# A fused attention and gated-MLP block on one core: V and the output projection in 64x128 tiles, weights loaded into both partition halves, new instruction lists

## The chip, the core and the metric

The kernel runs on one core of a Trainium2 chip. A core has TensorE (matmuls and transposes; PE in the profile, its weight loads PEld), VectorE (DVE), ScalarE (ACT) and GpSimd (POOL), and SyncE (SP), which here only issues DMAs. Each takes its instructions in the order of its own list and waits on semaphores for the others. Matmul operands lie in SBUF on 128 partitions; results go to PSUM, which has eight banks of 2 KB per partition. The metric is device time in microseconds (us) of one execution, lower is better.

## What is computed

2048 tokens x of width 448 in bf16; a dilated local attention, then a gated MLP that mixes over tokens:

```python
# attention: 16 heads of 28, window W = 8, dilation 2
q, k, v = layernorm(x) @ wqkv
idx = s - 2 * arange(8)                      # masked where negative
h = x + (softmax(q . k[idx] * 28**-0.5) @ v[idx]) @ wo
# gMLP: F = 1792, Fh = 896
z = gelu(layernorm(h) @ w_in)
z1, z2 = z[..., :Fh], layernorm(z[..., Fh:])
g = w_sp @ z2 + b_sp[:, None]                # over the tokens, 2048 x 2048
out = h + (z1 * g) @ w_out
```

## The kernel before

The tokens are split into two halves s of 1024. A unit u (0 to 7) is the blocks u and u + 8 of 128 tokens, one of each half. LayerNorm 1 of a unit takes, per block, a bn_stats (L818) and a bn_aggr (L819) on VectorE, a reciprocal root on POOL (L808, L809) or ScalarE (L830, L831), and a normalising tensor_scalar (L838). The unit is then transposed into xh: on TensorE with a copy out of PSUM (L854; units 0 to 2), or by a transposing DMA of SP (L845; units 3 to 7, and all units of LayerNorm 2). In xh, partition 64*s + f holds feature f of a 64-feature chunk c (seven chunks) of half s. So a matmul with 64 rows works on one half, and two such matmuls, one per half, run beside each other in the array. Each needs its weights on the same 64 partitions, so every weight is wanted in both partition halves. Before, each of wq, wk, wv and w_in is loaded into partitions 0 to 63 and copied into the others by VectorE or ScalarE (L803, L805; "cp" and "cpw" tasks). wq and wk come to a staging area in z2p and are spread from 28 to 32 columns per head on the way.

q and k are made in pieces of tokens per half: 0 to 128, 128 to 256, 256 to 512, 512 to 1024 (k runs 14 further back for the halo, from a separately normalised xhalo). The matmuls are 64x128 (L965), two groups of 128 columns to a task in the narrow pieces.

Attention goes in nine tiles of 114 queries per half. As the dilation is 2, even and odd tokens do not meet; each tile is handled by parity w, 64 keys and 58 query columns each. V of a tile (L1005) is made in four 64x64 tiles, half s by parity w, with every second token of xh as the stationary operand. Then come logits (L1040, 32x64 tiles), exp (L1053), a mask (L1060), row sums (L1069) and the product with V (L1089, both 64x32 tiles), ln and exp(-ln) of the sums (L1077, L1099), and the scaling "ot" (L1107), which writes over qT. There four heads lie on 128 partitions, so the output projection "y" (L1143) takes for each block four full 128x128 matmuls of 448 columns. "h" (L1151) adds x.

LayerNorm 2 follows per unit, then z2 (L1163, 64x128 tiles), gelu (L1173), LayerNorm 3 (L1179 to L1193); z1 (L1207) and its gelu (L1217); then g (L1244), bias and gate (L1254, L1262) and the output (L1273, L1281, L1285). The last stage is a dense run of 448 full matmuls for g and 112 for the output.

What order all this runs in is written out: `SEQ` holds five lists of task numbers, for SP, POOL, VectorE, ScalarE and TensorE. `replay` walks them with assumed durations only to choose PSUM banks and buffers, and semaphores are made from reads and writes. PSUM is taken in four pairs of banks by q, k, V, logits, sums, products, y, z2 and z1. The lists of before put the weight loads on ScalarE's queue (k, then q, and V later) and hold back all x blocks of units 2 to 7 until block 8 has landed. On TensorE they run unit 0 and 1 transposes, the eight narrow q and k tasks, the unit 2 transpose, then V and logits of tiles 0 and 1, the 256-wide pieces, and so on; the last q and k piece starts after tile 2's logits.

Of the kernel before, what the change touches and what calls it, by code (L numbers as in the profile page):

```python
# [24 lines left out]
QW = ST + 4  # L25

BF16 = mybir.dt.bfloat16
F32 = mybir.dt.float32
I32 = mybir.dt.int32
# [5 lines left out]
WPEN = 200  # L35
MPEN = 10.704
OFF = {"q": -124.25, "v": 1265.42, "evv": 569.01, "l": -1263.94, "exp": -259.78, "mask": -1085.83, "r": -1027.56, "o":
       -1264.27, "ln": 1046.18, "ot": 511.44, "y": -65.14, "h": 108.86, "ln2": -195.97, "z2": -1857.43, "ge": 2334.62,
       "n3": 1020.58, "x0": -60.60, "xd": 242.96, "evq": 1087.78, "cp": 975.37, "td": 561.22, "cw": -627.08}
ADJ = ()  # L40
SEQ = (
# [30 lines left out]
)  # L72
O_AFTER_LN = True
NBANKS = 8
TU = 26.48
NE = 2
NL = 2
NV = 3
SET_E = "natural_log_exp_and_others"
SET_G = "gelu_apprx_tanh_and_others"  # L80

# [122 lines left out]
class Task:  # L204
    __slots__ = ("name", "eng", "dur", "emit", "deps", "prio", "acq", "rel", "mode", "epoch",
                 "gate", "nbytes", "start", "end", "succ", "ndep", "rt", "nmm", "alts", "bw", "setup", "waits", "mark")

    def __init__(self, name, eng, dur, emit, deps=(), prio=0.0, acq=(), rel=(), mode=None,
                 epoch=None, gate=None, nbytes=0, nmm=0, alts=None):
        self.name = name  # L210
        self.eng = eng
        self.dur = dur
        self.emit = emit
        self.deps = [d for d in deps if d is not None]
        self.prio = prio
        self.acq = list(acq)
        self.rel = list(rel)
        self.mode = mode
        self.epoch = epoch
        self.gate = gate  # L220
        self.nbytes = nbytes
        self.nmm = nmm
        self.bw = 215.0
        self.setup = 2.0
        self.waits = []
        self.mark = None
        self.alts = alts
        self.start = self.end = None
        self.succ = []
        self.ndep = 0  # L230
        self.rt = 0.0


class Planner:


    ENGS = ("sp", "pool", "dve", "act", "pe")

    def __init__(self, pools, epochs, table_task, marker):
        self.tasks = []  # L240
        self.named = {}
        self.filler = None
        self.marker = marker
        self.pools = {k: [(0.0, s) for s in v] for k, v in pools.items()}
        self.epochs = epochs
        self.table_task = table_task
# [7 lines left out]
    def pick(self, p, n):  # L254

        free = {s: f for f, s in self.pools[p]}
        if p != "ps":
            return sorted(sorted(free, key=lambda s: (free[s], s))[:n]) if len(free) >= n else None
        whole = sorted((b for b in range(0, 32, 2) if b in free and b + 1 in free), key=lambda b: max(free[b], free[b + 1]))
        if n == 1:  # L260
            single = sorted((s for s in free if s ^ 1 not in free), key=lambda s: free[s])
            if single:
                return [single[0]]
# [1079 lines left out]
```

## Time and profile before

| | us |
|---|---|
| median of 3 runs | 246.23 (245.85 to 247.01) |
| profiled execution, first to last instruction | 247.4 |
| profiled execution's own time around that span | not recorded |
| TensorE busy | 232.1 (94%) |
| VectorE, ScalarE, POOL busy | 143.3, 91.4, 28.8 |
| first q matmul starts | 12.38 |
| last q and k piece starts | 40.17 |
| z1 starts | 93.26 |
| g starts | 126.5 |

In the profile a row is a line of the kernel, the engine and the operation, with what it writes and reads, its shape, and how often it occurs; then its busy time and the mean time of one. Engines overlap, so busy times do not add up to the span. The chain that ended last is followed back from the last instruction, at each step to what it waited for. A row of a stretch gives its length, then busy time and number of instructions for PE, PEld, DVE, ACT and POOL, then the granted TensorE clock (1.00 is full), the DMA engines' mean share and GB/s. Matmuls overlap in the array: one of 448 columns takes 349 ns from start to end while the next starts 94 to 190 ns after it, so work is counted from start to next start.

### The profile page before, as it was taken

How to read it: one execution, taken by the hardware profiler on the slowest of the kernel's cores; microseconds unless marked ns; L12 is line 12 of the kernel's file. 1: busy time of each engine (PE TensorE's matmuls, PEld its weight loads, DVE VectorE, ACT ScalarE, POOL GpSimd, SP SyncE). 2: the span in 40 equal slices, each digit the busy share in tenths (PEclk: the TensorE clock that was granted, in tenths of full speed). 3: DMA queues.
4: the chain of work that ended last, by engine and by line, in shares of the span. 5: the costliest groups of instructions: out<-in, count | busy, mean ns of one | idle time of the engine just before them, and what ended most of it. 6: DMA issues, size and time to landing. Idle time of an engine off the chain costs nothing.

```text
span 247.4 us, 6649 instructions
## 1 busy us (share of the span) xinstructions
PE 232.1 (94%) x3004; PEld 123.7 (50%) x3004; DVE 143.3 (58%) x281; ACT 91.4 (37%) x103; POOL 28.8 (12%) x69
## 2 busy tenths in 40 slices
PE   0399799999999999999999999999999999999995
PEld 0297485445556555555544444444444444444442
DVE  6697847779999897798970022335021407541743
ACT  2668784886979965575740000000000000000000
POOL 2843010000021112104530000000000000000000
DMA  6935965893224976886733333100000000010113
GB/s 159 255 80 61 138 91 98 128 154 71 46 40 85 152 197 124 180 147 150 108 85 85 87 85 85 42 3 0 0 0 0 3 0 0 2 46 29 56 57 111
DMA packets 54436, 20.02 MB, mean 81 GB/s; under 512 B 46584, under 2 KB 54280, under 8 KB 54408
## 3 DMA queue, kind: packets, MB, share of 16 engines
q1 hardware_dynamic: 52584, 18.05, 37.4%
q10 hardware_dynamic: 1824, 1.55, 2.8%
q8 instruction: 23, 0.38, 0.7%
q14 instruction: 5, 0.04, 0.1%
HBM read 6.39 MB, written 1.84 MB: 33 GB/s over the span
## 4 chain that ended last, share of the span: by engine, by line
PE 93%; DMA 3%; issue 1%; ACT 1%; ACTq 1%; DVE 0%
PE psum L1244 39%; PE psum L965 11%; PE psum L1163 9%; PE psum L1273 9%; PE psum L1207 9%; PE psum L1005 5%; PE psum L1143 5%; DMA z2p<-in_A_wqkv_dram 3%; PE psum L1040 3%; PE psum L1089 2%; PE psum L1069 1%; ACT reg L803 1%; ACTq L723 1%; ACT xh L803 0%; ACTq L730 0%
## 5 line engine op out<-in xcount | busy, mean ns | idle before, releaser
L1254 DVE TENSOR_TENSOR ub<-psum,reg 128x512 bf16<-128x512 f32 x28 | 18.8, 687 | 64.3 <-PE psum L1244 64.2
L1244 PE MATMUL psum<-reg,z2p 128*128 128x512 bf16 x224 | 50.0, 379 | 0.0
L1244 PE MATMUL psum<-wspT_lo,z2p 128*128 128x512 bf16 x224 | 49.0, 379 | 0.0
L1244 PEld LDWEIGHTS psum<-wspT_lo,z2p 128*128 128x128 bf16 x224 | 21.8, 98 | 26.6 <-issue 0.4
L1244 PEld LDWEIGHTS psum<-reg,z2p 128*128 128x128 bf16 x224 | 21.9, 98 | 26.1
L965 PE MATMUL psum<-xh,reg 64*128 64x128 bf16 (+3 forms) x448 | 28.5, 290 | 2.8 <-issue 2.0
L965 PEld LDWEIGHTS psum<-xh,reg 64*128 64x128 bf16 x448 | 19.4, 105 | 10.5 <-issue 3.4
L1163 PE MATMUL psum<-w_in,xh 64*128 64x448 bf16 x224 | 22.5, 349 | 0.0
L1273 PE MATMUL psum<-reg 128*128 128x448 bf16 x112 | 22.3, 352 | 0.0
L1207 PE MATMUL psum<-xh,w_in 64*128 64x512 bf16 x196 | 22.2, 376 | 0.0
L818 DVE BATCH_NORM_STATS2 st<-x_tm 128x6 f32<-128x448 bf16 x32 | 19.5, 609 | 1.0 <-DMA x_tm<-in_A_x_dram 0.8
L1179 DVE BATCH_NORM_STATS2 st<-z2p 128x6 f32<-128x448 bf16 x32 | 17.7, 612 | 2.6 <-ACT z2p L1173 2.5
L803 ACT ACTIVATE reg<-psum 128x896 bf16<-128x896 f32 (+3 forms) x21 | 16.8, 824 | 5.8 <-PE psum L965 4.2
L1053 ACT ACTIVATE reg<-psum 128x928 bf16<-128x928 f32 x18 | 16.1, 943 | 6.4 <-PE psum L1040 6.4
L1281 DVE TENSOR_TENSOR tring<-psum,x_tm 128x448 bf16<-128x448 f32 x16 | 9.6, 616 | 14.0 <-PE psum L1273 14.0
L808 POOL TENSOR_SCALAR rs<-mv 128x2 f32<-128x2 f32 x21 | 6.3, 300 | 93.7 <-DVE mv L819 78.4
L1173 ACT ACTIVATE z2p<-psum 128x896 bf16<-128x896 f32 x16 | 14.2, 916 | 6.8 <-PE psum L1163 6.8
L1163 PEld LDWEIGHTS psum<-w_in,xh 64*128 64x128 bf16 x224 | 11.9, 94 | 9.5 <-issue 0.9
L1217 ACT ACTIVATE reg<-psum 128x1024 bf16<-128x1024 f32 x14 | 13.7, 1030 | 7.8 <-PE psum L1207 7.8
L1273 PEld LDWEIGHTS psum<-reg 128*128 128x128 bf16 x112 | 11.0, 98 | 10.6
L1207 PEld LDWEIGHTS psum<-xh,w_in 64*128 64x128 bf16 x196 | 11.1, 94 | 9.7
L809 POOL TENSOR_TENSOR rs<-rs,nhalf 128x2 f32<-128x2 f32 x21 | 15.6, 743 | 1.8
(63 smaller groups left out, 201.2 us busy)
## 6 DMA issues: line engine op xcount, KB each, us to landing
out_dram<-tring SPq DMA_DIRECT2D x16, 112.0 KB, 1.7
x_tm<-in_A_x_dram SPq DMA_DIRECT2D x13, 112.0 KB, 5.7
w_in<-in_B_w_in_dram SPq DMA_DIRECT2D x2, 448.0 KB, 5.5
z2p<-in_A_wqkv_dram ACTq DMA_DIRECT2D x2, 392.0 KB, 6.3
reg<-in_B_w_out_dram SPq DMA_DIRECT2D x1, 784.0 KB, 4.8
w_in<-in_B_w_in_dram SPq DMA_DIRECT2D x2, 336.0 KB, 5.1
reg<-in_B_b_sp_dram SPq DMA_DIRECT2D x1, 512.0 KB, 4.2
reg<-in_A_wo_dram SPq DMA_DIRECT2D x4, 98.0 KB
```

Of the source, the lines that this page charges most:

```text
L803: iss("act", lambda e: e.activation(dst, src, AF.Copy), reads=rd, writes=wr)
L809: iss("pool", lambda e: e.tensor_tensor(dst, dst, nh, ALU.pow), reads=rr + [r_nhalf], writes=rr)
L818: iss("dve", lambda e: e.bn_stats(st[:, b, :], x_tm[:, b, :]), reads=[r_x[b]], writes=[rl[b]])
L965: iss("pe", lambda e, c=c, s=s, gi=gi, lhs=lhs: e.matmul(psum[:, bk[s] * 512 + cw * gi:bk[s] * 512 + cw * gi + cw], lhs, xh[64 * s:64 * s ...
L1053: iss("act", lambda e: e.activation(E[:, es[0], 2 * n:2 * n + 2, :], pair_view(lb, 0, 8 * JW), AF.Exp, scale=SCALE), reads=[r_bank[lb[0]], ...
L1163: iss("pe", lambda e, c=c, s=s: e.matmul(psum[:, zb[s] * 512:zb[s] * 512 + D], xh[64 * s:64 * s + 64, c, HX + 128 * u:HX + 128 * u + 128], ...
L1173: iss("act", lambda e: e.activation(z2p[:, u:u + 9:8, D * k:D * k + D], pair_view(zb, 0, D), AF.Gelu_apprx_tanh), reads=[r_bank[zb[0]], r_ ...
L1179: iss("dve", lambda e, b=b: e.bn_stats(st3[:, b, k, :], z2p[:, b, D * k:D * k + D]), reads=[r_z2[b][k]], writes=[r_st3[b][k]])
L1207: iss("pe", lambda e, c=c, s=s: e.matmul(psum[:, bk[s] * 512:bk[s] * 512 + 512], w_in[64 * s:64 * s + 64, c, 128 * f:128 * f + 128], xh[64 ...
L1244: iss("pe", lambda e, b=b: e.matmul(psum[:, gb[0] * 512:gb[0] * 512 + 512], z2p[:, b, 128 * f:128 * f + 128], src[:, b, 512 * (tc % 2):512 ...
L1254: iss("dve", lambda e: e.tensor_tensor(ub[:, us_[0], :], psum[:, gb[0] * 512:gb[0] * 512 + 512], bb[:, 512 * tc:512 * tc + 512], ALU.add), ...
L1273: iss("pe", lambda e, f=f: e.matmul(psum[:, wb[0] * 512:wb[0] * 512 + D], z1p[f][:, 128 * m:128 * m + 128], w_out[:, f, :], start=(f == 0) ...
```

## The change

1. V: VectorE or ScalarE first copies a tile's 128 tokens of xh into a small buffer xv, even tokens first. TensorE then takes 14 matmuls of 64x128 for V instead of 28 of 64x64.
2. Output projection: the two halves of the tokens get their own 64 partitions in oT (two heads each), wo is loaded twice (wo2), and y takes 16 matmuls of 64x128 instead of 8 of 128x128. Row sums and the product with V write to the matching partitions; the row sums of tile 0 take 8 matmuls instead of 16.
3. wq, wk, wv and w_in are loaded by two DMAs each, one per partition half. For wq, wk and wv one comes from SP and one from ScalarE's queue. The copies between halves go; four spreading copies for q and k stay, over 128 partitions.
4. q and k come in three pieces: 0 to 256, 256 to 512, 512 to 1024.
5. The mask is applied per half of the heads (two instructions for one); logits use 28 rows instead of 32; two bn_aggr stand together behind both bn_stats.
6. xhalo and thalo move into the staging area, ub into attention's region, memsets of wo and thalo from VectorE to POOL. The older search code goes.
7. The lists are new. Read by names, SP issues x0, x1, xhalo, x6, wq (half 0), x3, x10, wk (half 0), seven more x blocks, wv (half 0), wo1, x13, then the transposing DMA of unit 3, x4, and those of units 7, 4, 5, 6, then w_in, wo and w_sp loads. ScalarE issues x9, x8 and the other halves of wq, wk and wv, with two reciprocal roots between the last two. VectorE: bn of blocks 0, 9, 1, 8, the halo, normalise, copy of q, halo, xh of unit 0, copy of k, then bn of other units, parity copies of tiles 0, 3 and 2 and the remaining normalises. TensorE: transposes of units 1 and 0, q and k of the first piece, V of tile 0, the unit 2 transpose, logits of tiles 1 and 0, the second piece with V of tiles 1 and 3 in between, row sums and products of tiles 0 and 1, V of tile 2, the last piece. Tiles then run in pairs (2 and 3, 5 and 4, 6, 8, 7) up to z2.

```diff
+CQ = [0, 256, 512, ST]
+CK = [0, 256, 526, ST + HALO]
...
+        def ld_w(p):
             c0 = "qkv".index(p) * D
+            t_w[p] = [dma(eng, "w%s%d" % (p, s), lambda e, s=s: e.dma_start(
+                w_ld[p][64 * s:64 * s + 64], A_wqkv[:, c0:c0 + D].rearrange("(c p) n -> p c n", p=64)),
+                D * D * 2, writes=[r_ld[p][s]], issue=0.65, bw=350.0) for s, eng in ((0, "sp"), (1, "act"))]
...
-                if p == "v":
-                    copy(tk[0].eng, wv[64:128], wv[0:64], [r_st[p]], [r_w[p][1]])
-                else:
-                    copy(tk[0].eng, wpd[p][64 * h:64 * h + 64, :, 256 * j:256 * j + 256].rearrange("p c (h d) -> p c h d", d=32)[:, :, :, 0:DH],
-                         w_st[p][:, :, 224 * j:224 * j + 224].rearrange("p c (h d) -> p c h d", d=DH), [r_st[p]], [r_w[p][h][j]])
+                    copy(tk[0].eng, wpd[p][:, :, 256 * j:256 * j + 256].rearrange("p c (h d) -> p c h d", d=32)[:, :, :, 0:DH],
+                         w_ld[p][:, :, 224 * j:224 * j + 224].rearrange("p c (h d) -> p c h d", d=DH), r_ld[p], [r_w[p][j]])
...
+            def em(a=a, xs=xs, rx=rx, tk=tk):
+                o = HX - HALO + a
+                copy(tk[0].eng, xv[:, xs[0], :, :].rearrange("p c (w j) -> p c w j", w=2),
+                     xh[:, :, o:o + 128].rearrange("p c (j w) -> p c w j", w=2), rx, [r_xv[xs[0]]])
...
                 for c in range(NC7):
-                    for w in range(2):
-                        for s in range(2):
-                            iss("pe", lambda e, c=c, s=s, w=w: e.matmul(
-                                psum[64 * w:64 * w + 64, bk[s] * 512:bk[s] * 512 + D],
-                                xh[64 * s:64 * s + 64, c, HX - HALO + a + w:HX - HALO + a + w + 127:2],
-                                wv[64 * s:64 * s + 64, c, :], start=(c == 0), stop=(c == NC7 - 1),
-                                tile_position=(64 * s, 64 * w)),
...
+                    for s in range(2):
+                        iss("pe", lambda e, c=c, s=s: e.matmul(
+                            psum[:, bk[s] * 512:bk[s] * 512 + D],
+                            xv[64 * s:64 * s + 64, xs[0], c, :],
+                            wv[64 * s:64 * s + 64, c, :], start=(c == 0), stop=(c == NC7 - 1)),
...
-                for s in range(2):
-                    for g in range(4):
-                        iss("pe", lambda e, s=s, g=g: e.matmul(psum[:, bk[s] * 512:bk[s] * 512 + D],
-                                                              qT[:, s, g, 128 * u:128 * u + 128], wo_p[:, g, :],
-                                                              start=(g == 0), stop=(g == 3)),
+                for x in range(8):
+                    for s in range(2):
+                        iss("pe", lambda e, s=s, x=x: e.matmul(psum[:, bk[s] * 512:bk[s] * 512 + D],
+                                                              oT[64 * s:64 * s + 64, x, 128 * u:128 * u + 128],
+                                                              wo2[64 * s:64 * s + 64, x, :],
+                                                              start=(x == 0), stop=(x == 7)),
```

More of the change, by code (lines that the diff above doesn't have):

```diff
@@ L78 @@
 NV = 3
+NGE = 3
+NTR = 4
+NXV = 2
+XV_ON = ("dve", "act")
+MASK_ON = ("dve",)
 SET_E = "natural_log_exp_and_others"
 SET_G = "gelu_apprx_tanh_and_others"
+SEQ = (
[30 rows of a table added]
+)
 class Res:
@@ L204, with __init__ @@
 class Task:
[L205 to L209, printed above, removed]
+    __slots__ = ("name", "eng", "occ", "alts", "emit", "deps", "acq", "rel", "mode", "epoch", "nmm", "nbytes", "bw", "setup",
+                 "waits", "mark", "start", "end")
+    def __init__(self, name, eng, occ, emit, deps=(), acq=(), rel=(), mode=None, epoch=None, nbytes=0, bw=0.0, setup=0.0, nmm=0,
+                 alts=None):
         self.name = name
         self.eng = eng
-        self.dur = dur
+        self.occ = occ
+        self.alts = alts
         self.emit = emit
         self.deps = [d for d in deps if d is not None]
-        self.prio = prio
         self.acq = list(acq)
@@ L252, in add, with fetch @@
         return t
[L254 to L263, printed above, removed]
-            return [whole[0]] if whole else None
-        if len(whole) < n // 2:
-            return None
-        return sorted(b + i for b in whole[:n // 2] for i in range(2))
-    LAT = {"pe": 0.2, "act": 0.16, "dve": 0.14, "pool": 0.06, "sp": 0.05}
-    SAME = {"pe": 0.0, "act": 0.09, "dve": 0.08, "pool": 0.0, "sp": 0.0}
-    FILL = (0.5, 0.3, 0.25)
-    SWITCH = 0.1
-    CHUNK, ASK, NEED = 256, 115, 435
-    FETCH = (0.95, 2.5)
-    def fetch(self, nmm, now, dur, commit=False):
+    def fetch(self, nmm, now, dur, commit):
         n, m = self.pe_n, 2 * nmm
         ka, kn, free, av, shift = self.k_ask, self.k_need, self.f_free, self.avail, 0.0
-        new = []
         while True:
@@ L287, in fetch @@
                 free = max(t + self.FETCH[0], self.landed - 0.3, free)
-                new.append(free + self.FETCH[1])
-                free += 1.1
+                av.append(free + self.FETCH[1])
+                free += self.FETCH[2]
                 ka += 1
@@ L335, in replay @@
             best = None
-            for e in engs:
-                if ptr[e] == len(queue[e]):
+            for k, e in enumerate(engs):
+                if ptr[k] == len(queue[k]):
                     continue
-                t = queue[e][ptr[e]]
+                t = queue[k][ptr[k]]
                 if any(d.end is None for d in t.deps):
                     continue
-                at = max([free[e]] + [d.end + (self.SAME if d.eng == e else self.LAT)[d.eng] for d in t.deps])
+                at = free[k]
+                if e == "pe" and t.mode != pe_mode:
+                    at += self.DRAIN
+                if e == "act" and t.epoch is not None and loaded != self.epochs[t.epoch]:
+                    at += self.TABLE
+                for d in t.deps:
+                    if not (e == "pe" and d.eng == "pe"):
+                        at = max(at, d.end + self.SEE[e])
                 for p, n, h in t.acq:
@@ L349, in replay @@
                 if at is not None and (best is None or at < best[0]):
-                    best = at, e, t
-            now, e, t = best
-            extra = 0.0
+                    best = at, k, e, t
+            assert best is not None, [queue[k][ptr[k]].name for k in range(5) if ptr[k] < len(queue[k])]
+            now, k, e, t = best
             if e == "act" and t.epoch is not None and loaded != self.epochs[t.epoch]:
@@ L1125, in ld_wsp @@
                 dst[:, b, :], B_w_sp[1024 * half:1024 * half + 1024, 128 * b:128 * b + 128], transpose=True),
-                128 * 1024 * 2, prio=prio, deps=deps, writes=[r_wsp[b][half]], after=extra, issue=1.2, bw=165.0, setup=1.25)
+                128 * 1024 * 2, deps=deps, writes=[r_wsp[b][half]], after=extra, issue=1.2, bw=165.0, setup=0.05)
         S_ORDER = [b for u in range(NU) for b in (u, u + 8)]
-        for n, b in enumerate(S_ORDER):
-            ld_wsp(b, 0, 3.0 + 0.01 * n)
+        for b in S_ORDER:
+            ld_wsp(b, 0)
         t_h = []
```

759 lines of the change are left out of this document (289 added, 470 removed), and 60 rows, old and new, of the table SEQ.

## The prediction

> **What bounds the kernel now.** I read the page first, then the chain in order of time, the stage sums, and the early loads.
>
> ```profile
> span 247.4 us, 6649 instructions
> PE 232.1 (94%) x3004; PEld 123.7 (50%) x3004; DVE 143.3 (58%) x281; ACT 91.4 (37%) x103; POOL 28.8 (12%) x69
> ...
> PE 93%; DMA 3%; issue 1%; ACT 1%; ACTq 1%; DVE 0%
> ```
>
> TensorE carries 93% of the chain that ends last: time is won by a shorter TensorE list or an earlier start, and lost by a new wait. The chain in order of time (start, length, what) shows where:
>
> ```profile
> 2.92 7.07 DMA z2p<-in_A_wqkv_dram
> ...
> 10.01 1.51 ACT reg L803
> 11.52 0.81 ACT xh L803
> ...
> 12.38 9.04 PE psum L965 x164
> ...
> 28.68 1.74 issue
> ...
> 70.90 1.62 PE psum L1143 x8
> ...
> 84.88 3.13 PE psum L1143 x16
> ```
>
> The head is a weight load, its copy and a copy of xh; dense matmuls begin at 12.38. One wait of 1.74 stands at 28.68. The projection row says what a change of tile shape costs: 8 matmuls take 1.62, but 16 in a row 3.13, so 0.11 belongs to the change that follows. Stage sums (length, then busy us of PE, PEld, DVE, ACT, POOL):
>
> ```profile
> 12.38:40.17 27.79, 25.78 (x799) 20.85 (x800) 21.31 (x46) 20.55 (x30) 5.78 (x14) 1.00 0.64 94
> 40.17:80.20 40.03, 39.90 (x1126) 21.56 (x1128) 33.44 (x42) 32.12 (x35) 2.27 (x6) 1.00 0.49 87
> ```
>
> From 40.17 (the first matmul over the last 512 tokens) TensorE is full, with VectorE at 84% and ScalarE at 80% beside it. Loads, same columns, the last being GB/s:
>
> ```profile
> 3.00:7.00 4.00, 0.00 (x0) 0.00 (x0) 3.69 (x11) 1.79 (x3) 0.67 (x2) 1.00 0.95 204
> 7.00:9.00 2.00, 1.50 (x14) 1.33 (x14) 1.15 (x4) 1.30 (x1) 1.62 (x5) 1.00 1.15 178
> 9.00:11.00 2.00, 0.21 (x2) 0.00 (x0) 0.97 (x2) 1.20 (x2) 1.62 (x7) 1.00 1.10 361
> 16.00:17.00 1.00, 1.00 (x26) 1.00 (x20) 0.97 (x5) 1.00 (x2) 0.48 (x4) 1.00 0.88 274
> ```
>
> 3 to 7 is the weights of ScalarE's queue, 9 to 11 blocks of x, 16 to 17 the V weight by itself. The last transposing DMA before 40.17 is issued at 35.15 and lands at 39.97; 40.17 hangs on it.
>
> **The change part by part.** On VectorE and ScalarE I take start to next start, about 0.1 below the page's duration: bn_stats 0.53, normalise 0.31, mask 1.035, ot 1.12, h 1.00; on ScalarE exp 0.84, 896 to 1024 wide copies 0.80 to 0.90.
>
> *TensorE work.* V in 64x64 tiles takes 1.45 each with its change of shape, 1.34 without; z2 (L1163), the same form as the new V, takes 1.32 for 14: 0.02 x 9 = 0.2. The new projection is 16 at z2's rate, 1.51, as now without its change. So the gain is in changes: following both lists by name, 51 fall to 34, 17 x 0.11 = 1.9, 0.9 of it before the last q/k piece, where TensorE waits anyhow, and 1.0 behind it. q/k: the 224 narrow matmuls took 9.04; at the warm 256-wide rate (84 in 4.69) the same columns take 6.2, but most of the difference is a cold start (14 pairs take 1.49 at first, 0.78 later) that the new list pays too. I give 0. The row sums of tile 0 lose 8 matmuls, 0.1. Logits with 28 rows for 32, the output side of attention and everything behind z1 stay as they are; ub moves into attention's memory, free 30 us before ub's first use: 0.
>
> *Loads.* Each weight half is loaded instead of copied: 0.80 MB more for q and k, 0.40 for V, 1.61 for w_in, 0.40 for A_wo. In issue order, 1390 KB go through the q pair and 2420 KB through the k pair, 1606 of these q and k weights. Landing = 2.0 + bytes/rate + 1.6 (the two weight loads of before, 874 and 1275 KB, fit at 204 with a lag of 1.4 and 1.7). At 204 throughout: q 10.4, k 15.5. At 361 throughout: 7.5 and 10.3. I take weights at 274 (the row of a weight load that nothing disturbs) and x at 361: q 8.1, k 11.7.
>
> *Start.* LayerNorm of units 0 and 1: four bn, two pairs of aggregates, the halo's and four normalises on VectorE from 3.13 end at 7.75. Transposes to 9.2, VectorE's copy of q (0.54) under them, ScalarE's (1.41) under the first q group, the halo's normalise 0.42, xh's copy 0.5 to 1.0: q starts at 10.1 to 10.6, not at 12.38. POOL's longer memset of wo (0.47 per 448 wide, so 1.9) ends its constants at 6.5, ahead of the first transpose, and what VectorE is spared (0.43 + 0.81 of memsets) lay before the first x landed: nothing. Filler matmuls come in neither kernel, as the memset they wait for is near the end of VectorE's list. On ACT the table load sits ahead of the second k half; that is inside the k bounds.
>
> *VectorE's list to the last normalise.* It is in order, and behind the copy of k's second half stand all other units. From there: copy 0.54, 12 bn 6.4, 6 pairs of aggregates 1.8, 12 normalises 3.7, three parity copies 1.5, one copy of xh 0.8, two half masks 1.04: 15.8. A parity copy has no row: 0.33 at the rate of the 1568-wide copy (0.542), 1.00 at h's rate for 896 out of PSUM; I take 0.5, nearer to the copy, which also runs from SBUF to SBUF. Before, VectorE idled 4.5 between 23 and 34 in three waits for ScalarE; I take 1.5 (0 to 4.5). Start 11.8, end 29.1 (before: 34.5). Then three transposing DMAs 1.3 apart, the last issued at 31.7, landed at 36.5 (3.0 to 4.8 each). The last q/k piece starts at 36.7; TensorE's own work would be there at 35.1. Before, 40.17 had tile 2's logits (0.64) and 0.27 of waiting ahead of it, so the like point is 39.3. **Gain 2.6**; bounds 35.1 (gain 4.2) and 40.4 (k at 15.5, loss 1.1).
>
> *From there to z1.* Before: 93.26 - 40.17 = 53.1. The new list has one z2 group less (-1.32), those logits (+0.64), 9 changes of shape less (-1.0), V -0.1: 51.3. ScalarE gets the V copy of tile 6, three more q/k copies and one parity copy (0.80 + 2.7 + 0.80) and loses a w_in copy (2.4): 32.1 becomes 34.0. VectorE loses three q/k copies, a V copy and a w_in copy (5.4) and gets four parity copies and seven split masks (2.3): 30.3. Both fit, yet exps of two tiles now queue in pairs behind the q/k copies while TensorE's list waits in order for the four pairs of PSUM banks. I take **2.0 of waits**, mainly at the parity tiles 4 to 8 and at y6 behind ot7; 0.3 (as before) to 5.0. SP: the first transposing DMA of LayerNorm 2 now stands behind six w_in loads and eight w_sp loads that wait for one another; before, the seventh w_sp is issued at 60.35, one more takes 3.3, four more w_in halves 1.5 to 2 each: 64 to 72. Its data are ready near 67 and needed at 78, less 4.5 to land: covered by 1.5 or more, and past that each us counts. A fetch wait like that at 28.68 lies in these bounds.
>
> *z1 to the end.* 247.4 - 93.26 = 154.1, plus the z2 group left over: 155.4. The w_sp loads end about 7 ahead of use.
>
> Sum: 36.7 + 51.3 + 2.0 + 155.4 = 245.4 against 247.4, a change of -2.0. The profiled span stands 1.2 above the median of 246.23 (its lead-in and end are not recorded), so -2.0 is taken from the median: **244.2**.
>
> [...]
>
> **The rivals.** *Gain eaten by waits in the attention stage:* 4 instead of 2. For it: ScalarE at 83% in a fixed order, TensorE waiting in order. Against: VectorE's work there falls by 3.1. 246.2, no change.
>
> *Slower: the two queues take turns.* SP's part of the k pair has 1390 KB on its own queue, so 2780 KB move first; at 204 it lands at 2.0 + 13.6 + 1.6 = 17.2, and VectorE stands at the copy of k for 5.4 longer. All other units wait behind it, so do the transposing DMAs and the last q/k piece: 249.6. The sign turns when k lands at 13.8, and 0.5% is lost from 15.0. For it: 178 GB/s at 7 to 9, when both queues moved data. Against: 361 after it.
>
> *More gain: TensorE's own list decides.* Last piece at 35.1 to 35.5, waits 0.3 to 1: 241.7.
>
> *Not as told:* the narrow q/k pieces were slow by themselves; then another 1 or 2 in the direction of the third rival.
>
> **How the numbers follow.** Forecast (243.2 to 245.0) 0.38; more gain 0.20; no change 0.20; slower 0.22. A measurement tells 0.5% (1.2) from nothing: faster 0.58, same 0.20, slower 0.22. Range: the ends 35.1 + 0.3 give 240.9, k at 15.5 gives 247.9, the turns 249.6; leaving out the outermost tenth each side, 241.3 to 248.9. The forecast's own range is 242.8 to 245.4.
>
> **What would show it.** First q matmul at 10 to 11; k landed by 12; last transposing DMA landed at 36 to 37 and the first 512-wide q/k matmul right behind it; V groups at 1.32 and y at 1.51 where a 64x128 group follows; gaps of TensorE between 37 and 90 that sum to 2; z1 starting near 90; 155 from there. Wrong would make it: k landing past 14, VectorE's parity copies at 1 us, PSUM waits over 4, or transposing DMAs held up on SP.

## The result, and the profile after

The changed kernel takes 259.01 us (median of 4 runs, 258.45 to 260.08) against 246.42 (4 runs) for the kernel before on the same chip: a ratio of 1.051, 95% interval 1.048 to 1.055. Ratios here and below leave out executions over 1.5% longer than the fastest of their kernel (one of six with win0 early, three of twelve with w_sp moved). The changed kernel is 12.6 us slower, where 2 us less were forecast. Its profiled execution spans 257.0 and took 258.70 itself.

The head of the page of the changed kernel: span, TensorE's row, the granted clock in 40 slices, and the shares of the chain that ended last.

```profile
span 257.0 us, 6304 instructions
...
PE 233.9 (91%) x2822; PEld 123.2 (48%) x2822; DVE 135.6 (53%) x286; ACT 89.8 (35%) x107; POOL 26.0 (10%) x67
...
PEclk9999999999779999999999999999999999999999
...
PE 75%; DVE 9%; DMA 7%; ACT 4%; issue 2%; SPq 2%; POOL 1%
```

TensorE's share of the chain falls from 93% to 75%, and two slices show a granted clock under full. The records behind that row begin at 16.0; they give 0.5 from 67.2 to 70.6 and from 74.0 to 77.4, 3.413 us each, and 1.0 everywhere else up to the last microsecond. The stages of the changed kernel (stretch, length, then busy us of PE, PEld, DVE, ACT and POOL, the clock, the DMA share, GB/s), cut at the first q matmul, the last q and k piece, z1 and g:

```profile
13.36:39.86 26.50, 23.70 (x560) 17.10 (x561) 20.22 (x49) 21.08 (x29) 4.45 (x13) 1.00 0.64 121
39.86:101.01 61.15, 55.33 (x1346) 32.32 (x1347) 42.88 (x71) 40.45 (x46) 4.86 (x11) 0.94 0.73 128
101.01:136.08 35.07, 34.75 (x339) 17.39 (x336) 27.73 (x75) 21.90 (x25) 10.72 (x22) 1.00 0.78 138
136.08:257.00 120.92, 118.05 (x562) 54.70 (x560) 38.79 (x76) 1.77 (x2) 0.00 (x0) 1.00 0.16 40
```

The second and the last of these stretches in the kernel before:

```profile
40.17:93.26 53.09, 52.95 (x1302) 28.47 (x1304) 45.37 (x65) 42.29 (x43) 4.63 (x10) 1.00 0.59 107
...
126.50:247.40 120.90, 118.05 (x562) 54.71 (x560) 40.22 (x79) 1.45 (x2) 0.00 (x0) 1.00 0.14 37
```

Against my sum (36.7, then 53.3 to z1, then 155.4) the last piece starts 3.2 late, the stretch to z1 takes 7.85 more, and the rest 0.6 more: 11.6 in all. Most of the loss is in the attention stage (61.15 against 53.09 before, with DMA at 128 GB/s against 107), and none in g and the output (120.92 against 120.90). What TensorE waited for between 37 and 101 (line, what ended the wait, total, times, longest):

```profile
PE psum L807 <- ACT reg L852: 2.7, 1, 2.7
PE psum L759 <- ACT reg L603: 1.6, 1, 1.6
PE psum L896 <- issue: 1.3, 1, 1.3
PE psum L807 <- issue: 1.2, 1, 1.2
PE psum L838 <- issue: 0.5, 1, 0.5
```

The second is the one ahead of the last piece (39.86). The first looks like the PSUM wait behind ScalarE's exp that I had feared. The timeline of the same place, first the matmul's row and then the weight loads of the same matmuls (start, length, what, idle before), speaks against it:

```profile
62.72 0.90 PE L838 MATMUL psum<-reg 28*64 28x58 bf16 x64
66.29 1.96 PE L807 MATMUL psum<-reg,xv 64*128 64x448 bf16 x14 [2.68 <-ACT reg L852]
...
63.59 0.09 PEld L807 LDWEIGHTS psum<-reg,xv 64*128 64x128 bf16 x1
66.29 0.68 PEld L807 LDWEIGHTS psum<-reg,xv 64*128 64x128 bf16 x9 [2.62 <-issue]
```

The group's first weight load ran at 63.59, right behind ScalarE's ln of tile 5 (62.59 to 63.54), which frees the pair of banks that V of tile 4 writes. Then neither a matmul nor the second weight load came for 2.6 us, and the weight loads' row says "issue": they waited for nothing that the profile shows. The exp at 65.12 to 66.07, which the matmul's row names, writes nothing that V of tile 4 needs; it is only the last thing that ended before the gap did. The kernel's semaphores say the same: the group's only wait is for ScalarE's 50th signal, which is that ln, and the exp gives the 53rd.

TensorE's instructions come by DMA: the changed kernel's trace has 22 transfers of kind "instruction" on queue q8, 16,384 bytes each, to 5,644 matmuls and weight loads (256.5 to a transfer; I count in 256), and their start times. Behind 109 us, where TensorE's list is all long matmuls, transfer number j (from 0) starts when TensorE is 121 to 175 instructions past 256 * j. In the attention stage:

| transfer | instructions past 256 * j at its start | start | gap of TensorE | instructions past 256 * j where the gap begins | gap's end less start |
|---|---|---|---|---|---|
| 4 | 330 | 44.08 | 45.84 to 46.37 | 439 | 2.29 |
| 8 | 432 | 63.41 | 63.62 to 66.29 | 437 | 2.88 |
| 9 | 256 | 71.03 | 72.25 to 73.53 | 436 | 2.51 |
| 11 | 414 | 81.21 | 82.51 to 83.69 | 434 | 2.48 |

All four gaps end 2.3 to 2.9 after a late start; before's single stall (28.68 to 30.42) ends 2.8 after one too (27.61). A late start is not enough: transfers 6 and 7 started 354 and 356 instructions past and left no gap. What the gaps share is the place where they begin. Of all gaps of 0.4 us or more behind 14 us in the fifteen profiles of this document, 33 begin when TensorE is 434 to 447 instructions past 256 * j and end 2.3 to 2.9 behind the start of transfer j; the profile puts 28 of them down to issue and five to ScalarE. The other 34 gaps begin elsewhere in a block, and all but one of them end with another engine's work or a landed load. So I take those 33 for stands of TensorE for its instructions. The plan in both kernels (`replay`) assumes numbers near the measured 256.5, 121 to 175, 434 to 447 and 2.3 to 2.9 us, `CHUNK, ASK, NEED = 256, 115, 435` and 2.5 us from a transfer's start to its use, and I took no term from it.

What holds transfer 9 up can be seen in two windows of the changed kernel's DMA, 64.75 to 71.00 and 71.00 to 72.20 (queue, kind: packets, MB, share):

```profile
DMA packets 1644, 1.19 MB, mean 191 GB/s; under 512 B 1132, under 2 KB 1644, under 8 KB 1644
...
q1 hardware_dynamic: 1644, 1.19, 99.7%
...
q1 hardware_dynamic: 481, 0.12, 44.4%
q8 instruction: 1, 0.02, 5.6%
```

For 6.2 us no instruction transfer starts, while halves of w_in (the last two issued at 63.3 and 64.0, landed at 69.2 and 71.3) and w_sp blocks move; transfer 9 starts at 71.03, as the last half is ending. Transfer 8, by contrast, ran from 63.41 to 64.71 while a half of w_in issued at 60.45 had yet to land (65.71). When a transfer was asked for is in no row, so how the loads delay it stays open.

### The profile page after: what moved, and what is told of

Its sections match the earlier page's. It is cut to its first block, busy times and chain, and to the rows that moved or that the text cites. A ratio compares the mean times of both kernels' runs of the same rounds, so it can differ in the third digit from the quotient of the medians.

```text
span 257.0 us, 6304 instructions
## 1 busy us (share of the span) xinstructions
PE 233.9 (91%) x2822; PEld 123.2 (48%) x2822; DVE 135.6 (53%) x286; ACT 89.8 (35%) x107; POOL 26.0 (10%) x67
## 3 DMA queue, kind: packets, MB, share of 16 engines
q10 hardware_dynamic: 1680, 1.43, 2.4%
## 4 chain that ended last, share of the span: by engine, by line
PE 75%; DVE 9%; DMA 7%; ACT 4%; issue 2%; SPq 2%; POOL 1%
PE psum L1049 38%; PE psum L1075 8%; PE psum L1015 6%; PE psum L951 5%; PE psum L972 5%; DMA x_tm<-in_A_x_dram 5%; PE psum L759 5%; PE psum L807 3%; DVE tring L641 2%; DVE st L617 2%; DMA xh<-tring 2%; PE psum L896 2%; PE psum L838 1%; DVE st L988 1%; DVE xv L605 1%
## 5 line engine op out<-in xcount | busy, mean ns | idle before, releaser
L1059 DVE TENSOR_TENSOR reg<-psum,reg 128x512 bf16<-128x512 f32 x28 | 18.8, 688 | 70.8 <-PE psum L1049 60.1
L759 PE MATMUL psum<-xh,reg 64*128 64x256 bf16 (+2 forms) x336 | 27.3, 317 | 1.8 <-ACT reg L603 1.6
L603 ACT ACTIVATE reg<-psum 128x1024 bf16<-128x1024 f32 (+2 forms) x24 | 21.3, 920 | 10.5 <-PE psum L807 5.3
L759 PEld LDWEIGHTS psum<-xh,reg 64*128 64x128 bf16 x336 | 16.6, 98 | 10.4 <-ACT reg L907 2.0
L617 DVE BATCH_NORM_STATS2 st<-x_tm 128x6 f32<-128x448 bf16 x32 | 18.8, 614 | 4.6 <-DMA x_tm<-in_A_x_dram 4.6
L807 PE MATMUL psum<-reg,xv 64*128 64x448 bf16 x126 | 15.1, 378 | 4.0 <-ACT reg L852 2.7
L972 PEld LDWEIGHTS psum<-w_in,xh 64*128 64x128 bf16 x224 | 12.8, 94 | 9.1 <-DMA xh<-tring 1.1
L1075 PEld LDWEIGHTS psum<-reg 128*128 128x128 bf16 x112 | 11.0, 98 | 10.6
L915 DVE TENSOR_TENSOR reg<-psum,reg 128x912 bf16<-128x912 f32 x9 | 10.8, 1225 | 9.6 <-ACT reg L907 8.2
L1015 PEld LDWEIGHTS psum<-xh,w_in 64*128 64x128 bf16 x196 | 10.3, 94 | 10.7 <-issue 0.2
L951 PE MATMUL psum<-reg 64*128 64x448 bf16 x128 | 15.0, 377 | 0.2 <-ACT reg L603 0.2
```

Of the source, the lines that this page charges most:

```text
L603: iss("act", lambda e: e.activation(dst, src, AF.Copy), reads=rd, writes=wr)
L617: iss("dve", lambda e: e.bn_stats(st[:, b, :], x_tm[:, b, :]), reads=[r_x[b]], writes=[rl[b]])
L759: iss("pe", lambda e, c=c, s=s, gi=gi, lhs=lhs: e.matmul(psum[:, bk[s] * 512 + cw * gi:bk[s] * 512 + cw * gi + cw], lhs, xh[64 * s:64 * s ...
L807: iss("pe", lambda e, c=c, s=s: e.matmul(psum[:, bk[s] * 512:bk[s] * 512 + D], xv[64 * s:64 * s + 64, xs[0], c, :], wv[64 * s:64 * s + 64, ...
L951: iss("pe", lambda e, s=s, x=x: e.matmul(psum[:, bk[s] * 512:bk[s] * 512 + D], oT[64 * s:64 * s + 64, x, 128 * u:128 * u + 128], wo2[64 * ...
L972: iss("pe", lambda e, c=c, s=s: e.matmul(psum[:, zb[s] * 512:zb[s] * 512 + D], xh[64 * s:64 * s + 64, c, HX + 128 * u:HX + 128 * u + 128], ...
```

## The experiments

**Theory F:** w_in loaded twice (8 DMAs for 4, 1.61 MB more, most of it in the attention stage) delays TensorE's instruction transfers; new lists that put many short matmuls in a row (64 instructions in 0.3 us) leave them little time; TensorE stands, and the clock is halved for the 3.4 us behind. **Rivals:** W, PSUM banks held by ScalarE, as the waits name it; S, the late start; C, the parity copies at 1.0 instead of 0.5.

The gaps, pieces and clocks in the table are those of one profiled execution of each run; the ratio is over its executions.

| run | ratio to before (95%) | last q/k piece | TensorE's gaps of 0.4 or more from there to z1 | half-clock stretches up to z1 |
|---|---|---|---|---|
| kernel before | 1 | 40.17 | none | 0 |
| changed kernel | 1.051 (1.048 to 1.055) | 39.86 | 0.52, 2.68, 1.28, 1.17 | 2 |
| w_in moved | 1.034 (1.027 to 1.040) | 41.44 | 1.05, 1.14, 1.05, 1.13 | 1, at 26 |
| weights first | 1.045 (1.036 to 1.054) | 38.14 | 1.94, 2.69, 1.69 | 1, at 39 |
| no parity copy | 1.039 (1.033 to 1.045) | 39.42 | 4.71 | 2 in a row |
| copy in order | 258.13 (one run; before 247.44) | 39.28 | 1.07, 4.64 | 2 in a row |
| w_in once | 1.031 (1.025 to 1.037) | 41.08 | 1.34, 0.40 | 1 |
| and weights first | 1.030 (1.019 to 1.040) | 39.44 | 0.92, 1.94, 0.42 | 0 |
| and burst split | 1.021 (1.014 to 1.027) | 39.06 | 0.51, 0.52, 0.41 | 0 |
| and start order | 1.019 (1.015 to 1.024) | 37.90 | 1.16, 0.41 | 0 |
| and win0 early | 1.012 (1.006 to 1.018) | 36.04 | 0.44, 0.40 | 0 |
| and w_sp moved (profile of a long execution) | 1.012 (1.008 to 1.016) | 36.80 | 0.64, 0.83, 2.21 | 1 |
| before, w_in twice | 1.046 (1.040 to 1.053) | 40.04 | 0.73, 2.18, 4.35 | 2 |
| before, three of four twice | 1.017 (1.012 to 1.022) | 39.53 | 1.63 | 1 |
| before, one stall | 1.012 (1.007 to 1.017) | 39.77 | 2.26 | 1 |

The gaps of 0.40 to 0.44 in the rows from "w_in once" to "and win0 early", and the 0.64 of the row below them, begin 320 or 332 instructions past 256 * j and end with VectorE's work; they are no waits for instructions.

### The same loads at other places

```diff
 SP: ... tD1_3, x4,
+    win1_00, win1_01, win1_10, win1_11,
     tD1_7, tD1_4, tD1_5, tD1_6, win0_00, ..., wsp0_2,
-    win0_11, wsp0_10, win1_00, win1_01, wsp0_3, wsp0_11, win1_10, ...
+    wsp0_10, wsp0_3, wsp0_11, win0_11, ...
```

> Only the order of DMAs on SP's queue changes: the four loads of w_in's second half (win1) go right behind x4, where the trace of the changed kernel shows DMA nearly idle from 25.6 to 30.6, and one load of the first half (win0_11) moves from 60.5 to behind the w_sp block at 74. Same transfers, same bytes, same lists on the other engines. Theory F (fetch): TensorE's gaps of 2.68, 1.28, 1.17 and 0.52 behind 39.86 are waits for its own instructions; the 16 KB instruction transfers that end them started 3.5 to 8.1 us after TensorE reached the place where undisturbed ones start, right after a w_in load had landed. Then the gaps at 63.6 and 72.3 vanish, no stretch has clock 0.5, and 2.7 + 1.3 + 2.8 (slow matmuls) = 6.8 less, of which a new collision may take one: 252 to 253.5. Rival W (the release that the profile names: PSUM banks held by ScalarE's exp, L852): nothing of that is touched, 258 to 260, or more if the transposing DMAs of units 4 to 7 come later.

Measured: 256.16 us, 3.5% over before instead of 5.1%. The gaps of 2.68 and 1.28 became 1.05 and 1.14, and the clock stayed at 1.0 behind 30. ScalarE's list and copies are those of the changed kernel and only loads have moved, so W falls. F is right in kind and too hopeful in size: four gaps of 1.1 remain, each beginning 434 to 437 instructions into a block and ending 2.4 to 2.7 behind the start of an instruction transfer that started late beside w_sp blocks, and the early loads pushed the last piece to 41.44. The profile puts three of them down to issue and one to ScalarE's exp, and in a run further down the gap at the same place to ScalarE's inverse of the row sums: the name changes while the place does not.

### Start and parity copies

```diff
 SP: x0, x1, xhalo,
+    wq0, wk0, x6, x3, x10, ...
-    x6, wq0, x3, x10, wk0, ...
```

> On SP's queue the q and k weight halves (wq0, wk0) go ahead of x6, x3 and x10; nothing else changes. In the changed kernel they landed at 11.73 and 14.93, the halves on ScalarE's queue at 7.70 and 10.16. Expected: q pair at 9 to 10, k pair at 11 to 13.5, first q matmul at 10.5 to 11.5 instead of 13.36, last q/k piece at 37 to 38.5 instead of 39.86. Theory F: the time falls by that 1.4 to 2.9, 256 to 257.6, unless the shift moves a w_in load onto another instruction transfer (then up to 1 more or less). Rival S (the late start is the main cause of the whole loss): 4 or more less, under 255.

```diff
-                copy(tk[0].eng, xv[:, xs[0], :, :].rearrange("p c (w j) -> p c w j", w=2), ...
+                pass
...
-                            xv[64 * s:64 * s + 64, xs[0], c, :],
+                            xh[64 * s:64 * s + 64, c, o:o + 128],
```

> The nine parity copies (xv) are left out, and V's matmuls take xh in its unsorted order, so V's rows stand in the wrong order: a price of the copy, not a version. It takes seven copies of 1.0 us off VectorE and two of 0.98 off ScalarE. Theory F: three of them stand ahead of the last normalise, so the last q/k piece comes 1.5 to 3 earlier, and behind it they are off the path: 256 to 257.5. Rival C (the copy costing 1.0 instead of 0.5 is the main cause): 5 or more less, 254 or under. If the gaps of TensorE behind 39.86 shrink though no DMA moved, theory F is weakened.

```diff
-                copy(..., xv[:, xs[0], :, :].rearrange("p c (w j) -> p c w j", w=2),
-                     xh[:, :, o:o + 128].rearrange("p c (j w) -> p c w j", w=2), ...)
+                copy(..., xv[:, xs[0], :, :], xh[:, :, o:o + 128], ...)
```

> The changed kernel with the parity copies taken without the sort (128 tokens as they stand, so V's rows are in the wrong order): same elements, unit stride on both sides. If the sort is what makes a copy of 896 elements cost 0.99 on VectorE, it costs 0.3 to 0.5 here; if the number of elements does, it stays at 0.9 to 1.0. ScalarE's two stay at 0.95 in both. The time: 0 to 2 less, from the three copies ahead of the last normalise.

Weights first: q starts at 10.48 as I had forecast for the changed kernel itself, and the last piece at 38.14. Yet the time stays 4.5% over before (258.39, past F's 256 to 257.6 too), as gaps of 1.94, 2.69 and 1.69 follow. S falls: what the start gains is lost again at the instruction transfers. Without the copies the last piece comes only 0.4 earlier, not 1.5 to 3, and a gap of 4.71 stands at V of tile 4, the place of the 2.68. The ratio falls from 1.051 to 1.039, about 3 of the 12.6 us, so the copies are a part of the loss, and a larger one than the last piece shows; how the rest comes about these runs don't settle. As the main cause, at 5 us or more, C falls. The waits of the kernel without copies show that place under its true name:

```profile
PE psum L806 <- issue: 4.7, 1, 4.7
```

The sort does make the copy dear. One copy of 896 elements on VectorE, of the changed kernel and of the one that copies in order (ns, least, median, most):

```profile
L605 DVE COPY xv<-xh x7: 1069/1079/1085, 16.4 to 79.9; 128x896 bf16<-128x896 bf16 x7
...
L604 DVE COPY xv<-xh x7: 600/612/626, 16.9 to 80.1; 128x896 bf16<-128x896 bf16 x7
```

In the order of the tokens the same 896 elements take 0.61 us instead of 1.08; ScalarE's two copies take 0.96 and 0.97. Taking the sort out moved the last piece by 0.6 (39.28).

### Doubled loads in the kernel before

```diff
                 ld_in.append(t)
+                # behind each w_in load, the same load again into an unused part of z2p
+                iss("sp", lambda e: e.dma_start(z2p[64:128, 7 * z + c0:7 * z + c1, :], B_w_in[...]), ...)
```

> The kernel before with each of its four w_in loads issued twice; the second goes to the other partition half of z2p, which nobody reads, and 1.61 MB more move at the places where before issues them (24, 42, 51 and 80). The copies between halves stay. Theory F: instruction transfers wait longer behind the doubled loads; before has one fetch wait, 1.74 at 28.68, and now 1 to 5 us of such waits, at 28.7 more, and near 45 to 57: 247.5 to 252. Rivals W, S and C: a doubled load is hidden, 246 to 247.

259.62 us, past F's 247.5 to 252, but 5.9 of the 10.4 us by which its span exceeds before's is an artefact: ScalarE's first gelu writes z2p and waited for the fourth extra load (4.35 at 89, and a half clock behind). Up to there it is 4.5 behind before. So the fourth was left single:

> The kernel before with the first three of its four w_in loads issued twice (1.23 MB more at 24, 42 and 51); the fourth, at 80, stays single. With all four doubled, ScalarE's first gelu waited for the fourth extra load, as it writes to the same memory: a wait of 4.35 at 89 that says nothing of instruction transfers. Up to there that run was 4.5 us behind before, by gaps of 0.73 and 2.18 and a half-clock stretch. Theory F: the same gaps near 48 and 60 and the half clock, no wait at 89: 3.5 to 5 us, 1.014 to 1.020 of before. If doubled loads as such are hidden, under 1.005.

252.69 us, 1.7% over before, inside F's 1.014 to 1.020 and far from the 1.005 of hidden loads. Its waits of TensorE from 25 to 101, and the clock:

```profile
PE psum L1053 <- issue: 1.8, 2, 1.6
PE psum L1102 <- issue: 1.8, 1, 1.8
...
PEclk9999999999799999999999999999999999999999
```

The 1.8 of L1102 stands at 36.9 and takes the place of before's 1.74 at 28.68. No other engine's list was touched, and 1.23 MB more bring a gap of 1.63 at 59 where there was none, a half clock from 62, and z1 3.2 later. This is the part of F that one run shows by itself: doubled loads alone cost 4 us, about a third of the loss.

### What a stall costs

```diff
+                        if (i, n, half) == (5, 1, 1):
+                            iss("pool", lambda e: e.memset(z2flat[:, 7168:11968].bitcast(F32), 0.0),
+                                reads=[r_bank[lb[0]]], writes=[r_gate])
...
-                                reads=[r_w["v"][s]] + rx, writes=[r_bank[bk[s]]])
+                                reads=[r_w["v"][s]] + rx + ([r_gate] if i == 4 else []), writes=[r_bank[bk[s]]])
```

> The kernel before with one deliberate stall of TensorE: behind the logits of tile 5 (59.8) GpSimd, idle there, fills an unused part of z2p (about 2.5 us, from 1.9 us for 1792 words), and V of tile 4 waits for it. It prices a stall like the 2.68 of the changed kernel by itself, with before's lists and transfers. Theory F with the clock: the 3.4 us stretch behind it is granted 0.5, and the stall costs 2.5 plus 1.0 to 1.7: 3.5 to 4.2 us, 1.014 to 1.017 of before. Rival: the half clock has another cause (the length or the mix of the changed kernel's work), the records stay at 1.0 and it costs 2.5 or less, 1.010 or under.

The wait came out at 2.26, and the next 3.413 us (61.4 to 64.8) were granted 0.5. The stretch from one group of the last q and k piece to z1, with the stall and in before:

```profile
43.55:96.41 52.86, 50.37 (x1219) 26.65 (x1213) 42.91 (x63) 40.71 (x41) 6.74 (x11) 0.97 0.57 101
...
43.95:93.26 49.31, 49.18 (x1218) 26.40 (x1212) 42.85 (x63) 40.71 (x41) 4.63 (x10) 1.00 0.60 108
```

3.55 longer for a stall of 2.26, in the longest of the six executions (252.52): the half clock adds 1.3. The record of 0.5 begins 0.6 ahead of the stall's end, when TensorE had stood for 1.64. Over the six the ratio is 1.012 (1.007 to 1.017), between F's 1.014 and the rival's 1.010, and the mean clock of the six is 0.992 or 0.993 in four, 0.998 and 1.000 in two; so the price of the half clock rests on the profile and not on the times. Here a stall of 2.26 had a half clock behind it, and in the other runs the halved stretches follow windows of 3.4 us with 0.9 to 3.4 us of standing, while windows with up to 1.8 were also let pass; a plain limit doesn't come out of these runs.

### Taking the causes away in turn

```diff
+ w_in's second partition halves: four copies by VectorE, two ahead of ot1, one behind evq2_0, one behind ot3
- four of eight w_in DMAs;  SP: ... x4, win1_00, win1_10, tD1_7, ... (win0_00 at 36 and win0_10 at 53 stay)
```

> From the changed kernel: w_in is loaded once, into partitions 0 to 63 (four DMAs instead of eight, 1.61 MB less), and VectorE copies it into the other half, in stretches where the trace shows it idle (two copies at 35 behind V's copy of tile 3, one at 50, one at 57; about 1.2 and 0.9 us each, from the 0.35 ns per element of the weight copy). The two loads of the second half stand behind x4 (25.6), the others where they were (36.9 and 52.5). Theory F: as with the moved loads the half-clock stretches behind 60 vanish; TensorE's gaps there fall under the 4.4 left with the moved loads (four of 1.05 to 1.14, each behind an instruction transfer that waited for a w_sp transpose), as fewer transfers are in flight: 3 to 4.4. Time 1.02 to 1.03 of before. Rival W (ScalarE's exps and PSUM): the gaps stay as in the changed kernel, 1.045 to 1.06, the more as VectorE gets 4.3 us of work.

```diff
 SP: x0, x1, xhalo,
+    wq0, wk0, x6, x3, x10, ...
```

> As with w_in loaded once, and the q and k halves ahead of x6, x3 and x10 on SP. Alone that order brought the last q/k piece from 39.86 to 38.14, but the time did not follow: 6.3 us of fetch gaps behind it and 3.4 us of half clock took its place. Theory F: with w_in out of the way the start's gain of 1.5 to 2 passes through: 1.01 to 1.025 of before and 1.5 to 2.5 us under the run without it. If the gaps grow by as much as the start gains, TensorE's list itself is bound by something later (w_sp or VectorE), and the start is worth nothing.

```diff
 TensorE: mmo5_0, mmr5, mmo5_1,
+         mmv4, mml4_1, mml6_0, mmy2, ...
-         mml4_1, mml6_0, mmv4, mmy2, ...
```

> As the run with w_in once and weights first, and on TensorE's list V of tile 4 goes ahead of the two logits tasks of tiles 4 and 6. In the changed kernel five tasks in a row (products and sums of tile 5, logits of tiles 4 and 6) run 272 instructions in 1.7 us just ahead of the first gap, so an instruction transfer asked for at their start cannot be there. Theory F: the gap at 63 (1.0 to 1.9 us) shrinks to under 0.5 as V's 1.5 us go by while the transfer runs, and the time falls by 0.5 to 1.5 against the run without it. Rival W: logits and exp of tile 4 come later, ScalarE waits, and the time rises by 0.5 to 1.

Loading w_in once gives 1.031, at the upper edge of what F expected and well off W's 1.045 or more, though VectorE has 4.3 us more to do; the gap of 1.34 was still followed by a half clock. Weights first on top of it brought the last piece forward by 1.6, but its gaps of 0.92 and 1.94 gave part of that back, and the median fell by 1.2 instead of 1.5 to 2.5 (254.13 against 255.33). Splitting the burst then took that gap to 0.52 and 1.6 us off. That fits the burst as the second half of the mechanism; the intervals of these three runs overlap, and only the gap itself is clear. The waits from 40 to 100 of the run with the split burst:

```profile
PE psum L844 <- issue: 1.0, 2, 0.5
PE psum L844 <- DVE x_tm L966: 0.4, 1, 0.4
...
```

```diff
 SP:      ..., x13,
+         x4, tD1_3, win1_00, win1_10, tD1_7, tD1_5, tD1_6, tD1_4, ..., tD2_3, wsp0_5, ...
-         tD1_3, x4, win1_00, win1_10, tD1_7, tD1_4, tD1_5, tD1_6, ..., wsp0_5, tD2_3, ...
 VectorE: cpk1,
+         xv0, bn1_3, bn1_10, bn1_6, bn1_5, bn1_11, ..., nrm1_15, nrm1_13, nrm1_14, nrm1_4, nrm1_12, four masks, xv2, ...
-         bn1_5, xv0, bn1_3, bn1_11, bn1_10, ..., xv2, nrm1_15, two masks, nrm1_13, nrm1_4, nrm1_14, nrm1_12, two masks, ...
```

> On top of w_in once, weights first and the split burst: x4 goes ahead of the first transposing DMA on SP; VectorE takes the statistics of block 5 later (it waited 1.5 for it) and does the last five normalises ahead of four half masks and the parity copy of tile 2; the transposing DMAs go in the order 7, 5, 6, 4; in the z2 stage the third unit's normalises come ahead of a statistic and of h, and one w_sp load behind a transposing DMA. Theory: the last q/k piece stood behind VectorE's list (last normalise at 32.05, of which 2.9 were waits for x5 and x4 and 2.3 work that could wait); it ends at 27 to 28, the last transposing DMA lands at 34 to 36, the piece starts at 36.5 to 37.5 instead of 39.06, and 1.5 to 2.5 us come off: 1.010 to 1.016 of before. If fetch gaps grow by as much, the shift met other transfers.

```diff
 SP: x4, tD1_3, win1_00, win1_10,
+    win0_00,
     tD1_7, tD1_5, tD1_6, tD1_4,
-    win0_00,
     wo0, ...
```

> As the run with the new start order, and the first w_in load of the z1 half (win0_00) goes from 36 to the stretch behind x4, where 0.9 MB move and DMA has room until 33. At 36 it holds an instruction transfer up by 6 to 7 us (asked for near 36 to 37, started at 43 to 44 in five kernels) and costs a gap of 0.4 to 0.9 at 45. Theory F: that gap goes, 0.4 to 0.9 less. Against it: the transposing DMAs of units 7, 5, 6 and 4 come behind it, each us that the last lands past 36.5 is lost; then 0.5 to 1.5 more.

```diff
 SP: ..., wsp0_10,
-    wsp0_3, wsp0_11, tD2_0, wsp0_4, wsp0_12, tD2_1, tD2_2, tD2_3, ...
+    tD2_0, wsp0_3, wsp0_11, tD2_1, wsp0_4, tD2_2, wsp0_12, tD2_3, ...
```

> As the run with win0 early, and two w_sp loads (wsp0_3 and wsp0_11) leave the stretch 58 to 65 for places behind the transposing DMAs of LayerNorm 2; from the ninth load on two may be in flight. Theory F: instruction transfers asked for near 56, 60 and 64 start 1.3 us after the place where they are asked for instead of 1.8 to 2.7, fewer executions meet a gap there, and the median comes nearer to the profiled span: 0 to 2 us less, 1.004 to 1.012 of before. Against it: w_sp blocks come to g late, with up to 2 us more.

The start order brought the piece to 37.90, and nothing in time (252.54 against 252.53): instruction gaps of 1.90 at 28.1, ahead of it, and of 1.16 at 40.7 came in. With win0_00 early as well the piece started at 36.04, no instruction gap of 0.4 or more stood behind it, and the time fell to 250.83; the profile is of this run's fastest execution (248.87), so the gaps of the others are not seen. Its stage from the last piece to z1:

```profile
36.04:90.91 54.87, 52.35 (x1349) 27.77 (x1346) 46.62 (x74) 42.06 (x48) 4.76 (x11) 1.00 0.61 87
```

54.87 for 61.15, at 87 GB/s for 128. Moving two w_sp blocks did no more: the median is 250.71, but executions range from 249.62 to 257.79, and the profile, of a long one, has a gap of 2.21 at 65.7 behind an instruction transfer that started at 65.26. The cause there is not settled. Of the 12.6 us these steps together give back about three quarters, and how that is shared among them is not shown; none of them beats the kernel before, whose lists remain 1.2% faster.

## Why the prediction was wrong

*Loads and start: wrong, 3.2 us.* The sum had q at 8.1 and k at 11.7 from a pair's bytes at 274 and 361 GB/s. The halves on ScalarE's queue landed at 7.70 and 10.16, those on SP's at 11.73 and 14.93, so the pair was late by SP's half, behind x6, x3 and x10. First q matmul 13.36, not 10.1 to 10.6; with the weights first it was 10.48. 14.93 lies past the 13.8 at which I had the sign turn, but neither "taking turns" (17.2) nor my rates give both queues. No run shows the even turns that the 17.2, and with it the 249.6 of the range, rests on: in the changed kernel ScalarE's queue moved 857 packets to SP's 271 from 3 to 7 us, 73 to 1151 from 8 to 13, and nearly as many, 441 to 479, only from 13 to 16.

*Parity copy 0.5: wrong,* 0.99 on VectorE, at the end of my bounds; the row of a copy with unit stride was the wrong neighbour. It moved the last piece by 0.4 to 0.6; the kernel without copies was about 3 us nearer to before, and where the rest of that comes from is open.

*VectorE's list and the last piece at 36.7: late at 39.86.* Weights first gave 38.14, so the loads are 1.7 of the 3.2. The run with the new start order and early win0 did it at 36.04. The last transposing DMA landed at 39.61, not 36.5.

*TensorE's list, 51.3 to z1: it fits the time that is left over.* V takes 1.43 (1.32 and a change of shape, as I had it; 1.45 before), y 1.62 and 1.51 in turn. 61.15 less the four gaps (5.65) and less what V of tiles 4 and 6 and y2 and y4 took over their usual 1.43 and 1.6 (2.8) is 52.7; the 1.4 over 51.3 is short waits.

*"I take 2.0 of waits, mainly at the parity tiles ... and at y6": the step that failed.* They were 7.0, and of another kind. I priced the doubled w_in loads only by what queues behind them on SP, and found that covered. I had the stall of 28.68 among the lines shown, called it a fetch wait, and put "a fetch wait like that" inside the bounds without asking what had made it: an instruction transfer started at 27.61, 4.5 after the end of the one ahead of it, with a w_in load issued at 23.98 and landed at 30.1. With more bytes and denser lists its kind had to be expected more often. The runs show stalls for instructions of 5.65 in all where I had ScalarE's banks: this is 5.0 of the 11.6 us.

*The clock: missing.* The stretches of before's profile all show a clock of 1.00, and no step allowed for a stall costing more than its length: 2.8 us.

*z1 to the end 155.4:* 156.0, right. *SP behind the w_in loads:* the first transposing DMA of LayerNorm 2 was issued at 76.4, later than the 64 to 72 I had, and landed at 80.9 for use at 89.8: covered, with z2 itself late.

*The anchor.* I compared a sum with before's profiled execution (247.4) and took the difference from the median, calling the span 1.2 above it. In every run that lists both, the time is 1.7 to 2.1 above the span; before's profiled execution therefore took about 249.3 (an estimate from those), 3 above the median, and part of its stall may be its own. Hence 9.6 us between the profiles and 12.6 between the medians.

*The rivals.* Waits in the attention stage was the right place, with the wrong engine and 4 us where there were 7 and the clock behind them. The slower rival had 249.6 by late weights; earlier weights gained nothing that is clear of the spread in the two runs that had them, so late weights alone explain little of the loss.

## What to carry to other kernels

Here TensorE's instructions were a load like any other, 22 transfers of 16 KB. Where a list has runs of short instructions (here 272 in 1.7 us) and the queues are busy, count what moves while its next block is due, and keep large transfers out of those stretches; a second load in place of a copy of 1.1 us was a bad trade here. A wait that the profile ascribes to an engine is checked against the weight loads of the same matmuls, the semaphore the group really waits for, and the count of instructions since the last block: five of 33 stalls for instructions bore ScalarE's name here. And a stall of TensorE in a dense stage can cost more than its length: 3.55 for 2.26 in the one run that priced it.

## What was not expected of the hardware

33 gaps of TensorE over fifteen profiles began 434 to 447 instructions past 256 * j and ended 2.3 to 2.9 us after the start of transfer j, of 16 KB. Such a transfer started up to 7.9 us after TensorE had reached the place where undisturbed ones start (transfer 9 of the changed kernel, with 1.19 MB of loads moving). A granted clock of 0.5 came in stretches of 3.413 us, or two of them, behind stalls as short as 1.28, and once behind 0.9 of short gaps. Of two equal loads of one weight, issued 1 to 3 us apart on two queues, the one on ScalarE's queue landed 4 to 5 us ahead (7.70 and 11.73, 10.16 and 14.93, 17.04 and 21.02); SP's queue had x blocks ahead of its own. What stays open: how loads delay an instruction transfer, and why the lists with early win0, which leave 0.84 us of gaps behind the last piece in their profile, are still 1.2% behind.
